# Batch-by-batch folding in a Fourier-mixing and low-rank-mixer kernel: where the first batch's narrow sums run, how the second batch's sine groups and channel step are computed, and when the third batch is folded

## The chip, the cores and the metric

The kernel runs on one core of a Trainium2 chip. A core has a matrix engine (TensorE, "PE" in the profile; its weight loads are listed as "PEld"), a vector engine (VectorE, "DVE"), an activation engine (ScalarE, "ACT"), a general engine (GpSimd, "POOL") and a queue engine (SyncE, "SP"). Each engine works through its own list of instructions in order; semaphores make one wait for another. Matmul results go to PSUM, everything else lives in SBUF. The metric is the device time of one execution in microseconds (us).

## The reference

```python
def _attn_ref(x):                       # x: 8 x 3136 x 256
    X = np.fft.fft(x, axis=1)
    X = np.fft.fft(X, axis=2)
    return X.real.astype(np.float32)

def _moe_ref(x, U, V, w_ch1, w_ch2):    # U: 3136 x 32, V: 32 x 3136
    xt = x.transpose(0, 2, 1)
    h = xt @ U @ V
    u = x + h.transpose(0, 2, 1)
    ch = np.maximum(u @ w_ch1, 0.0) @ w_ch2     # 256 -> 1024 -> 256
    return (u + ch).astype(np.float32)
```

The output is `_moe_ref` of `_attn_ref(x)`: the real part of a two-dimensional Fourier transform of each of eight batches, then a low-rank mixing along the sequence and a two-layer product along the channels, both with a residual.

## The kernel before

**Batches.** Each of the 8 batches has 3136 rows. Its inputs (`xf`, the rows read forwards, and `xr`, read backwards; 98 partitions of 8 rows each, plus row 0 in partition 98) are folded by `fold(b)`: `along_d` (line 386) adds or subtracts mirrored channels into `EOF_` and `EOR_`, `mirror` (L395) joins these into `EOS`, `half` (L399) joins the two halves of the sequence into `G[b % 2][par]`. The next batch's loads (`load_half`, L55, L86, L101, L103) are issued by GpSimd from inside the fold, since they overwrite what the fold has read. From batch 1 to batch 7 a fold has 16 steps, or 14 where there is no next batch to load. For batches 0 and 1 there is also a narrow column (channel 0, handled alone; L392).

`transform(b)` then runs the sequence transform: eight calls of `seq`, one for each parity `par`, type `typ` (1 is cosine, 0 sine) and input parity `pn`. A plain call is four matmuls of 425 columns (L485); with `pn == 0` ScalarE evicts the result to an `ev` tile (L489), with `pn == 1` VectorE adds and subtracts it and `ev` into the tiles `A` (cosine) and `B` (sine) (L492, L500, L504). `halves` (L425 to L437) replaces a `pn == 0` call: its four matmuls (L430) have 229 columns only, because the outputs mirror each other, and two VectorE instructions (L436, L437) make the full `ev` from the two sums. `quarters` (L439 to L464) goes one step further and is used from batch 2 (`B0`).

Then comes the channel step, from `A` and `B` to `S` and `T`. `chan` (L628) makes one of the two with two matmuls of 392 columns (L631 from `A`, L633 from `B`) and one copy out of PSUM (L635, ScalarE, or VectorE where `dve` is set). `even_ch` and `odd_ch` make both at once: one product of `A` (L643), evicted by ScalarE to `evd` (L645), one product of `B` (L652), and two VectorE instructions that add and subtract (L654). With them goes `across` (L664, L666), which copies 64 rows of `A` into `VA`, tied behind the last Relu on ScalarE; without them `last_row` (L684) writes a single row of `VA` on VectorE. Batch 0 and 1 use `chan`, batches 2 to 7 `even_ch` and `odd_ch`.

`first_channel` (through `narrow`, L545 to L577) makes a narrow row of `VA` for batches 0 and 1: 16 matmuls (L556), an eviction to `evc` (L560), and six sums (L570, L573, L574), on VectorE for batch 0 and on GpSimd for batch 1. On GpSimd it needs a second eviction, `evo` (L563), because there the sums read SBUF. The same routine makes the narrow rows of batches 2 to 7 together (`column_steps`). All tiles `ev`, `evc`, `evo` and `evd` share four buffers; all PSUM tiles of these steps share three (`dft`).

**Chunks.** The second stage works on 49 chunks of 512 rows. `front(c)` adds a product of `TA` and `VA` (L709) to `S` or `T` and writes `u` (L725, two or more VectorE instructions); a DMA transposes it. `first_product(c, j)` (L735, two matmuls of 512 columns, Relu on ScalarE L737) runs for j = 0 to 7; `second_product(c-1, t)` (L751, eight matmuls of 256 columns) for t = 0 to 3, with three VectorE additions to the output tile after each pair (L757, L759, L760).

**Order.** Step `8 * c + j` runs one first product, on odd j one second product of the chunk before, then what `due` lists for this step, and at j = 3 the front of the next chunk. `spread(steps, lo, hi)` puts a fold or a transform evenly over the steps lo to hi. Batch 1's first output row lies in chunk 6, whose front is issued at step 43; batch 2's in chunk 12 (step 91). Up to the end of chunk 0 the order of each engine is as written; from chunk 1 on a planner orders the instructions by what it takes to be ready, while the fold's instructions keep their place (`pin`).

## Time and profile before

| what | value |
|---|---|
| time, median of 3 runs | 447.03 us (446.45 to 447.28) |
| time of the profiled execution | 447.31 us |
| its span in the profile | 445.2 us |
| mean granted TensorE clock | 1.00 |
| VectorE busy | 353.1 us |
| ScalarE busy | 297.5 us |
| GpSimd busy | 85.7 us |

The span runs from the first to the last instruction that the profile shows; 2.1 us of the execution's own time lie outside it. A line of a timeline gives the start, the duration, the engine, the source line, the operation, output and inputs, shapes, and the number of instructions merged into the line; in square brackets, how long the engine stood idle before it and what ended that. TensorE's matmuls overlap, so a matmul's listed duration is longer than its share of the engine: that share is the distance from one start to the next.

### The profile page before, as it was taken

How to read it: one execution, taken by the hardware profiler on the slowest of the kernel's cores; microseconds unless marked ns; L12 is line 12 of the kernel's file. 1: busy time of each engine (PE TensorE's matmuls, PEld its weight loads, DVE VectorE, ACT ScalarE, POOL GpSimd, SP SyncE). 2: the span in 40 equal slices, each digit the busy share in tenths (PEclk: the TensorE clock that was granted, in tenths of full speed). 3: DMA queues.
4: the chain of work that ended last, by engine and by line, in shares of the span. 5: the costliest groups of instructions: out<-in, count | busy, mean ns of one | idle time of the engine just before them, and what ended most of it. 6: DMA issues, size and time to landing. Idle time of an engine off the chain costs nothing.

```text
span 445.2 us, 8087 instructions
## 1 busy us (share of the span) xinstructions
PE 435.7 (98%) x2960; PEld 316.4 (71%) x3012; DVE 353.1 (79%) x838; ACT 297.5 (67%) x564; POOL 85.7 (19%) x144
## 2 busy tenths in 40 slices
PE   8999999999999999999999999999999999999997
PEld 6456766776677777777777777777777777777775
DVE  8879998888998799878998789878998776443433
ACT  8857747565885669655875569655876569656562
POOL 8973217300931002300211001300000000000000
PEclk9999999999999999999999999999999999999999
DMA  7998997995199437674779537782333332434343
GB/s 133 210 230 180 229 173 117 245 153 103 49 230 265 120 106 216 190 171 73 157 203 222 108 103 216 196 167 71 95 119 95 91 100 73 117 97 121 93 125 112
DMA packets 103249, 65.36 MB, mean 147 GB/s; under 512 B 73806, under 2 KB 99624, under 8 KB 100464
## 3 DMA queue, kind: packets, MB, share of 16 engines
q1 hardware_dynamic: 97528, 39.10, 40.1%
q0 software_dynamic: 5664, 25.75, 21.6%
q8 instruction: 23, 0.38, 0.3%
q14 instruction: 16, 0.13, 0.1%
q10 hardware_dynamic: 18, 0.00, 0.0%
HBM read 29.33 MB, written 25.69 MB: 124 GB/s over the span
## 4 chain that ended last, share of the span: by engine, by line
PE 91%; DVE 2%; DMA 2%; issue 1%; POOL 1%; ACT 1%; DVEq 0%; POOLq 0%
PE p L751 38%; PE p L735 35%; PE pt L485 6%; PE ph L709 5%; DMA xb<-in_x_dram,xidx 2%; PE ptq L446 2%; PE pst L643 1%; PE pst L652 1%; PE m L850 1%; PE ptc L556 1%; ACT h L737 0%; DVE eor L386 0%; PE pst L631 0%; DVE eof L386 0%; PE pst L633 0%
## 5 line engine op out<-in xcount | busy, mean ns | idle before, releaser
L737 ACT ACTIVATE h<-p 128x512 bf16<-128x512 f32 x392 | 222.0, 597 | 119.5 <-PE p L735 107.3
L735 PE MATMUL p<-u,w 128*128 128x512 bf16 x735 | 209.3, 379 | 1.2 <-DVE B L500 0.2
L751 PE MATMUL p<-w,h 128*128 128x256 bf16 x1568 | 203.0, 273 | 1.4
L751 PEld LDWEIGHTS <-h 128*128 128x128 bf16 x1568 | 153.2, 98 | 50.4 <-DVE o L760 0.3
L735 PEld LDWEIGHTS <-w 128*128 128x128 bf16 x784 | 106.1, 144 | 35.1 <-issue 2.0
L757 DVE TENSOR_TENSOR o<-p,ut 128x4 f32<-128x4 f32 (+1 forms) x100 | 16.2, 162 | 54.9 <-PE p L751 53.3
L759 DVE TENSOR_TENSOR o<-p,ut 128x254 f32<-128x254 f32 (+1 forms) x100 | 40.5, 405 | 0.0
L760 DVE TENSOR_TENSOR o<-p,ut 128x254 f32<-128x254 f32 (+1 forms) x100 | 40.5, 405 | 0.0
L468 POOL TENSOR_TENSOR tab<-tf 128x64 bf16<-128x64 f32 x7 | 3.1, 440 | 179.2 <-DVE tf L492 179.1
L386 DVE TENSOR_TENSOR eof<-xf 99x1024 bf16<-99x1024 f32 x28 | 35.8, 1293 | 0.0
L386 DVE TENSOR_TENSOR eor<-xr 99x1024 bf16<-99x1024 f32 x28 | 34.8, 1247 | 0.0
L725 DVE TENSOR_TENSOR u<-ph,S 128x512 bf16<-128x512 f32 (+23 forms) x63 | 34.3, 553 | 0.0
L725 DVE TENSOR_TENSOR u<-ph,T 128x512 bf16<-128x512 f32 (+23 forms) x63 | 34.2, 553 | 0.0
L55 POOL DMA_INDIRECT xf<-in_x_dram,xidx x14 | 17.3, 1234 | 62.0 <-DVE eof L386 48.5
L709 PE MATMUL ph<-va,ta 128*128 128x512 bf16 (+15 forms) x124 | 28.6, 328 | 0.3
L485 PEld LDWEIGHTS <-g 98*128 98x128 bf16 (+1 forms) x152 | 14.7, 98 | 13.1 <-issue 0.7
L395 DVE TENSOR_TENSOR eos<-eof,eor 99x1024 bf16<-99x1024 bf16 (+1 forms) x28 | 19.2, 702 | 0.0
L654 DVE TENSOR_TENSOR S<-evd,pst 128x392 bf16<-128x392 f32 (+1 forms) x24 | 13.5, 564 | 6.4 <-PE pst L652 4.1
L485 PE MATMUL pt<-tabs,g 98*128 98x425 bf16 x80 | 17.6, 344 | 0.0
L457 DVE TENSOR_TENSOR ev<-ptq,ex 128x131 f32<-128x131 f32 (+1 forms) x24 | 6.9, 289 | 12.9 <-ACT ex L450 12.9
L399 DVE TENSOR_TENSOR g<-eos 99x2048 bf16<-99x2048 bf16 (+1 forms) x14 | 16.9, 1217 | 0.0
L485 PE MATMUL pt<-tabc,g 98*128 98x425 bf16 x72 | 15.5, 344 | 0.0
(198 smaller groups left out, 381.0 us busy)
## 6 DMA issues: line engine op xcount, KB each, us to landing
out_dram<-o SPq DMA_DIRECT2D x48, 512.0 KB
xr<-in_x_dram POOLq DMA_DIRECT2D x14, 784.0 KB, 8.2
xb<-in_x_dram POOLq DMA_DIRECT2D x2, 392.0 KB, 7.9
ut<-u SPq DMA_TRANSPOSE x49
w<-in_moe_w_ch_dram POOLq DMA_DIRECT2D x1, 512.0 KB
out_dram<-o SPq DMA_DIRECT2D x4, 128.0 KB
va<-in_moe_V_dram POOLq DMA_DIRECT2D x2, 196.0 KB
w<-in_moe_w_ch_dram POOLq DMA_DIRECT2D x1, 256.0 KB, 7.2
```

The costliest lines, as they stand in the source:

```text
L55: nc.gpsimd.indirect_dma_start(out_, None, bass.AP(t.tensor, t.offset, [[w, rows], [1, w]]), bass.IndirectOffsetOnAxis(idx, 0), element_of ...
L386: pin(nc.vector.tensor_tensor(dst[:, a, :, part * P:(part + 1) * P].rearrange("p i (k t) -> p i k t", k=2), lo, hi, op=AL.subtract if part ...
L395: pin(nc.vector.tensor_tensor(EOS[:, a, :, cols], EOF_[:, a, :, cols], EOR_[:, a, ::-1][:, :, cols], op=op))
L399: pin(nc.vector.tensor_tensor(G[b % 2][par][:, :, cols], EOS[:, 0, :, cols], EOS[:, 1, :, cols], op=AL.add if par == 0 else AL.subtract))
L485: nc.tensor.matmul(pt[:], g[:kp(i), i, P * typ:P * (typ + 1)], tabs[typ][:kp(i), i, par, :], start=(n == 0), stop=(n == NI // 2 - 1))
L709: nc.tensor.matmul(ph, TA[b % 2][:k, s * P:(s + 1) * P], VA[b % 2][:k, lo:hi], start=start, stop=True)
L725: nc.vector.tensor_tensor(u[:, s, col:col + hi - lo], ph[:, col:col + hi - lo], src, op=AL.add)
L735: nc.tensor.matmul(p1[:], W1[:, s, j::JT], k["u"][:, s, :], start=(s == 0), stop=(s == 1))
L737: LAST[0] = nc.scalar.activation(k["h"][:, j, :], p1[:], AF.Relu)
L751: nc.tensor.matmul(p2[:, t % w, :], h[:, j, rs], W2[:, j, :], start=(j == 0), stop=(j == JT - 1))
L759: nc.vector.tensor_tensor(o[:, ts, 1:P], p2[:, :w, 1:P], ut[:, ts, 1:P], op=AL.add)
L760: nc.vector.tensor_tensor(o[:, ts, P + 1:D], p2[:, :w, P + 1:D], ut[:, tT, P - 1:0:-1], op=AL.add)
```

## The change

Four things change together.

- The first batch's narrow sums go from VectorE to GpSimd (`eng=nc.gpsimd`), which adds the `evo` eviction and moves all six sums, two of them (the late ones) to behind the start of chunk 0.
- The second batch's two sine groups (`typ == 0`) with `pn == 0` go through `halves`, as its cosine groups did already.
- The second batch's channel step uses `even_ch`, `odd_ch` and `across` in place of eight `chan` calls; `last_row(1)` goes, the low product of batch 1 reads all 128 rows of `TA` and `VA`, and one of the two memsets of `VA[1]` goes.
- Batch 1's fold is spread over steps 2 to 21 (was 4 to 23) and its transform over 21 to 42 (was 23 to 42); batch 2's fold over 30 to 58 (was 24 to 55) and its transform over 60 to 90 (was 57 to 90).

```diff
-        if pn == 0 and (b >= B0 or b == 1 and typ == 1):
+        if pn == 0 and b:
             (quarters if b >= B0 else halves)(d, g, par, typ)
             return
...
-        k = P if b >= B0 else 2 * R + 1
+        k = P if b else 2 * R + 1
...
             for ch in range(4):
-                for h in range(2):
-                    yield lambda ch=ch, h=h: chan(b, ch * 392 + (1 if ch else 0),
-                                                  (ch + 1) * 392 + 1, h)
+                yield lambda ch=ch: (even_ch(b, ch), across(b, ch, False))
+                yield lambda ch=ch: (odd_ch(b, ch), across(b, ch, True))
             yield from row[3:]
-            yield lambda: (lowrank(b), last_row(b))
+            yield lambda: lowrank(b)
             return
...
-    narrow_0 = list(first_channel(0, tag=("p2", 2), late=late))
+    narrow_0 = list(first_channel(0, tag=("p2", 2), late=late, eng=nc.gpsimd))
...
-    va_zeros(1)
+    nc.gpsimd.memset(VA[1][R:2 * R].bitcast(I32), 0)
...
         if b == 1:
-            spread(list(fold(b)), 4, 23)
-            spread(list(transform(b)), 23, hi)
+            spread(list(fold(b)), 2, 21)
+            spread(list(transform(b)), 21, hi)
         else:
-            spread(list(fold(b)), hi - 66, hi - 35)
-            spread(list(transform(b)), hi - 33, hi)
+            lag = 3 if b == B0 else 0
+            spread(list(fold(b)), hi - 66 + 2 * lag, hi - 35 + lag)
+            spread(list(transform(b)), hi - 33 + lag, hi)
```

## The prediction

> **What bounds the kernel now.** I read the busy shares and the chain of waits first, then busy time by stretches, then the timelines where the change works.
>
> ```profile
> PE 435.7 (98%) x2960; PEld 316.4 (71%) x3012; DVE 353.1 (79%) x838; ACT 297.5 (67%) x564; POOL 85.7 (19%) x144
> PE 91%; DVE 2%; DMA 2%; issue 1%; POOL 1%; ACT 1%; DVEq 0%; POOLq 0%
> ```
>
> TensorE is busy for 98% of the span and makes 91% of the chain that ends last. So a matmul column less is time less, as long as nothing starves TensorE. What could starve it is VectorE, third of the busy columns here (the columns are stretch, its length, then busy us of PE, PEld, DVE, ACT, POOL with counts, clock, DMA share, GB/s):
>
> ```profile
> 54.00:62.00 8.00, 7.95 (x54) 5.40 (x54) 7.86 (x18) 4.40 (x9) 0.07 (x1) 1.00 1.13 211
> 62.00:70.00 8.00, 7.79 (x61) 5.02 (x61) 7.42 (x17) 3.92 (x9) 2.53 (x4) 1.00 0.70 140
> 70.00:78.00 8.00, 7.80 (x51) 5.38 (x50) 6.86 (x12) 6.55 (x15) 7.76 (x9) 1.00 0.70 114
> 86.00:94.00 8.00, 7.95 (x58) 6.10 (x58) 5.83 (x12) 4.72 (x9) 0.00 (x0) 1.00 1.05 204
> 118.00:126.00 8.00, 7.88 (x54) 5.76 (x53) 8.00 (x15) 6.89 (x14) 6.98 (x7) 1.00 0.52 123
> ```
>
> From 54 to 70 us, in batch 1's transform, VectorE has 0.7 us free in 16; at 118 it has none; at 86 it has 2.2 of 8. ScalarE has room everywhere. TensorE's clock is 1.00 throughout. The change takes work from TensorE in the stretch where VectorE is full and gives VectorE more: that is the question of this case.
>
> **TensorE: what goes.** Distances from one start to the next:
>
> ```profile
> 54.62 0.56 PE L430 MATMUL pth<-tabc,g 98*128 98x229 bf16 x4
> 55.02 0.88 PE L485 MATMUL pt<-tabc,g 98*128 98x425 bf16 x4
> 55.74 0.89 PE L485 MATMUL pt<-tabs,g 98*128 98x425 bf16 x4
> ...
> 68.15 0.33 PE L631 MATMUL pst<-A,mc 128*128 128x393 bf16 x1
> 68.32 0.33 PE L633 MATMUL pst<-B,msn 128*128 128x393 bf16 x1
> 68.49 0.59 PE L735 MATMUL p<-u,w 128*128 128x512 bf16 x2
> ```
>
> A plain group of four takes 55.74 - 55.02 = 0.72 us, a `halves` group 55.02 - 54.62 = 0.40. Two sine groups: 2 x 0.32 = 0.64. A channel product takes 68.32 - 68.15 = 0.17; eight `chan` calls are 16 of them, the even and odd products 8: 8 x 0.17 = 1.36. Together 2.00 us. The low product over 128 instead of 65 rows costs nothing: its columns stay, and columns set the time of every row above.
>
> **VectorE, ScalarE, GpSimd: what comes.**
>
> ```profile
> L654 DVE TENSOR_TENSOR S<-evd,pst 128x392 bf16<-128x392 f32 x18 | 10.1, 563 | 4.0 <-ACT h L737 2.0 <-PE pst L652 1.8
> L437 DVE TENSOR_TENSOR ev<-pth,ev 128x229 f32<-128x229 f32 x2 | 0.8, 398 | 0.0
> L684 DVE TENSOR_TENSOR va<-S,T 1x1567 bf16<-1x1567 bf16 x2 | 1.9, 968 | 0.9 <-ACT T L635 0.9
> L645 ACT COPY evd<-pst 128x392 f32<-128x392 f32 x18 | 8.7, 481 | 0.1
> L664 ACT COPY va<-A 64x392 bf16<-64x392 bf16 x18 | 9.3, 515 | 0.4
> L395 DVE TENSOR_TENSOR eos<-eof,eor 99x1024 bf16<-99x1024 bf16 x26 | 17.9, 703 | 0.0
> L759 DVE TENSOR_TENSOR o<-p,ut 128x254 f32<-128x254 f32 x96 | 39.4, 411 | 0.0
> ```
>
> VectorE in batch 1: 8 additions and subtractions x 0.563 = +4.5; two each of L436 and L437, at most 4 x 0.398 = +1.6; `last_row(1)` -1.0: +5.1 us. The last two rows are used further down. ScalarE: 4 evictions x 0.481 + 8 copies x 0.515 = 6.0, for eight copies of 392 columns out of PSUM, 8 x 0.481 = 3.8: +2.2 us. In the 70 to 78 stretch it has 1.45 of 8 free and more on both sides, so I put it at nothing; without that room it would delay Relus by up to 2.2.
>
> Against the +5.1 stands batch 2's fold, moved away. Before step 43, where batch 1 is first needed, the old spread (24 to 55, 16 steps) puts 11 fold steps, the new one (30 to 58) 8: three `along_d` fewer, at 1.2 to 1.8 us each:
>
> ```profile
> 69.46 1.02 POOL L573 TENSOR_TENSOR va<-evo,evc 1x393 bf16<-1x393 f32 x1
> 70.44 1.47 POOL L574 TENSOR_TENSOR va<-evc,evo 1x392 bf16<-1x392 f32 x1
> ...
> 73.89 1.82 DVE L386 TENSOR_TENSOR eof<-xf 99x1024 bf16<-99x1024 f32 x1
> 76.57 0.97 DVE L684 TENSOR_TENSOR va<-S,T 1x1567 bf16<-1x1567 bf16 x1 [0.85 <-ACT T L635]
> 80.02 1.21 DVE L386 TENSOR_TENSOR eor<-xr 99x1024 bf16<-99x1024 f32 x1
> ```
>
> That is -3.6 to -5.4, and -1.2 for the two late sums that leave VectorE at 32.75. So the sum up to step 43 is between +0.3 and -1.5 us. It has to come out 1.8 us sooner than now, because the handover has no slack:
>
> ```profile
> 83.81 0.61 DVE L725 TENSOR_TENSOR u<-ph,T 128x448 bf16<-128x448 f32 x1
> 84.60 0.81 PE L735 MATMUL p<-u,w 128*128 128x512 bf16 x3
> ```
>
> Chunk 6's `u` is done at 84.42, TensorE takes it at 84.60: 0.18 us, and TensorE will ask 2.0 earlier. VectorE's idle 0.85 before `last_row(1)` goes with that instruction. -0.85 and -0.6 (the middle of the sum) are 1.45 of the 1.8 wanted; I charge the rest, +0.3.
>
> One line above gives a price that the change pays: a GpSimd sum takes 1.02 alone and 1.47 beside VectorE's fold, and an `along_d` 1.82 beside GpSimd against 1.21 alone. The Trainium skill ("SBUF — State Buffer", Who interferes with whom) makes it a rule against this change: a VectorE instruction with two SBUF inputs and a GpSimd instruction that reads SBUF exclude each other, and the later one blocks fully. By that rule each overlap would cost up to a whole 1.0 to 1.2 us; the rows show 0.45 and 0.6, so the trace agrees in kind and gives half the price. By the rule's price the forecast would be about 1 us higher.
>
> **The start.** The narrow sums leave VectorE ahead of its join at 28.87 (four) and at 32.75 (two).
>
> ```profile
> 25.53 3.02 PE pt L485 x16
> 28.87 0.04 DVE tab L468
> ...
> 25.58 0.51 ACT L560 COPY evc<-ptc 64x425 f32<-64x425 f32 x1 [0.48 <-PE ptc L556]
> ...
> 30.07 0.59 PE L709 MATMUL pu<-va,ta 65*128 65x512 bf16 x2
> 38.80 0.67 POOL L86 DMA_DIRECT2D xr<-in_x_dram  x1 [7.51 <-DVE eor L386]
> ...
> L570 POOL TENSOR_TENSOR tf<-evo,evc 1x32 f32<-1x32 f32 x2 | 0.7, 368 | 5.5 <-ACT evo L563 5.4
> ```
>
> The first four gain nothing: the chain runs through TensorE's sixteen matmuls to 28.55. They must not cost either: the evictions, at 25.58 and, new, 26.1, end at 26.6; GpSimd needs 0.37 + 1.02 + 0.37 us to the end of the second short sum, 28.4, which the join at 28.87 reads; the second row is done at 29.4, and L709 reads it at 30.07. The slack is 0.5 to 0.7 us; if it is gone, each tenth of lateness costs a tenth. VectorE's sums of that moment read PSUM and only one tile in SBUF, so I expect no stretching. What waits behind on GpSimd (memsets, `ME`, the narrow casts of L392, batch 2's first load) shifts by the six sums, 4 x 1.02 + 2 x 0.37 = 4.8 us; that load now stands 7.51 us idle ahead of its issue at 38.80, which covers it.
>
> But the fold's two earlier steps are not free. Steps 2 and 3 lie ahead of chunk 1's front, in the part whose order is as written:
>
> ```profile
> 32.75 1.22 DVE L574 TENSOR_TENSOR va<-evc,ptc 1x392 bf16<-1x392 f32 x2
> 35.30 0.68 DVE L725 TENSOR_TENSOR u<-ph,T 128x512 bf16<-128x512 f32 x1
> 35.90 2.35 DVE L386 TENSOR_TENSOR eor<-xr 99x1024 bf16<-99x1024 f32 x2
> ...
> 36.66 0.33 PE L631 MATMUL pst<-A,mc 128*128 128x392 bf16 x1
> ```
>
> Two `along_d` (2.35) now stand before `u`, in place of two sums (1.22): `u` ends 1.13 later, at 37.1. TensorE wants it at 36.23, two 512-column matmuls ahead of the last row (0.17 x 512 / 393 = 0.22 each). Bounds: 0 (the planner fills the hole with other matmuls) to 0.9, and with both `along_d` stretched by the moved sums' company 0.9 + 1.2 = 2.1. I take +0.3, nearer the filled case, because from chunk 1 on channel products and second products stand ready.
>
> **Batch 2 later.** The old trace loses time where batch 3's fold meets GpSimd's column sums:
>
> ```profile
> 113.04 3.25 DVE L386 TENSOR_TENSOR eof<-xf 99x1024 bf16<-99x1024 f32 x2
> ...
> 117.30 0.33 PE L643 MATMUL pst<-A,me 128*128 128x392 bf16 x1 [0.36 <-DVE T L654]
> ...
> xr<-in_x_dram POOLq DMA_DIRECT2D x14, 784.0 KB, 8.2
> ```
>
> TensorE idles 0.36 us. That fold does not move. Batch 2's transform does, from 57 to 60, into this full stretch by about one `seq`: between -0.4 (the meeting shifts apart) and +1.1 (one more stall of a `seq`'s two VectorE sums); I take 0. Its fold then ends some 3 steps later; 94 us is its deadline and the stretch at 86 has 2.2 us free. The eight loads of batch 3 that it issues move by 4 to 6 steps behind GpSimd's narrow sums; they land in 8.2 us (the last row) and are first read at 113: nothing; without those 20 us of lead the wait would be VectorE's.
>
> **The sum:** 447.31 - 2.00 + 0.3 (handover) + 0.3 (start) = 445.91 for the profiled execution; that execution is 0.28 above the median of the runs shown, so 445.63. Two gains were set to nothing in it: the 0.36 at 117, and what TensorE misses of the 62 to 78 stretch (15.59 busy of 16, 0.4 us), where the ScalarE copies out of PSUM that go are thickest. I count half of them, 0.4, and put the forecast at 445.2 us.
>
> **The rivals.**
> *All of it and the stalls too:* the start's hole is filled, the handover holds, and both of these stalls go in full. 447.03 - 2.0 - 0.8 = 444.2. For it: those stalls are VectorE's and ScalarE's evictions, which change. Against: VectorE has no more room than before.
> *No change:* the start costs its upper 0.9 and the handover slips by 1.0: 447.03 - 2.0 + 1.9 = 446.9. It is what a zero slack at both places would do.
> *VectorE becomes the bound in steps 31 to 42 (slower).* The sum up to step 43 balances, but its end does not: these 11 steps now hold 8 x 0.563 = 4.5 of S and T, four `along_d` of 1.2 that GpSimd's sums stretch by 0.6 each (7.2), two mirrors (1.4), output additions (nearly three pairs of 2 x 0.41, 2.3) and `u` (about three of 0.68, 2.0): 17.4 us. TensorE's work there is 11 steps of two 512-column and four 256-column matmuls (2 x 0.22 + 4 x 0.11 = 0.88), 1.4 for the channels and some 0.7 for fronts and low rank: 11.8 us. Odd products keep their PSUM tile until both sums are done, and the fold keeps its place, so TensorE would wait. Of the 5.6 about 1.6 (two pairs of output additions) fit into the output sums' two buffers: +4.0, 447.03 - 2.0 + 4.0 = 449.0. It makes the kernel slower from 2.9 us of new stalls on. Against it: the planner can let late channel products wait, as only the first 448 rows are due at step 43.
>
> **How the numbers follow.** A measurement of this kernel tells about 0.2% (0.9 us) from no change. Forecast (444.5 to 446.1): 0.55; all of it and stalls: 0.12; no change: 0.14; slower: 0.19. Faster 0.67, same 0.14, slower 0.19. The range runs from 443.9 to 448.2, into the slower case; the forecast's own is 444.5 to 446.1.
>
> **What would show it.** Right: L430 twice as often, L485 fewer by 8, L631 and L633 only batch 0's; chunk 6's `u` and TensorE within 0.3 us near 82.6; the sixteen matmuls' end still near 28.5. Wrong: TensorE idle before chunk 1's first product, or before L643 and L652 between 60 and 80; ScalarE waiting on GpSimd's hold on `evc` and `evo`; idle over 1 us at 105 to 130.

## The result: the changed kernel is 4.1% slower

| what | before | after |
|---|---|---|
| time, median | 447.02 us (446.45 to 447.73) | 464.84 us (464.31 to 467.61) |
| ratio after / before | | 1.0413, interval 1.0383 to 1.0442 |
| time of the profiled execution | 447.31 us | 464.86 us |
| its span | 445.2 us | 463.1 us |
| mean granted TensorE clock | 1.00 | 0.985 |

The forecast was 445.2 us, in a range up to 448.2. The time lies 17.8 us above the kernel before and far outside that range. Medians and brackets take all executions of a kernel; a ratio can leave out executions more than 1.5% above the fastest.

The page of the kernel after, busy time and chain of waits by engine:

```profile
PE 437.4 (94%) x2951; PEld 317.2 (68%) x3004; DVE 352.7 (76%) x843; ACT 300.6 (65%) x569; POOL 91.6 (20%) x149
PE 80%; DVE 7%; DMA 4%; POOL 4%; issue 2%; ACT 2%; SPq 0%; DVEq 0%; POOLq 0%; ACTq 0%
```

TensorE is busy for as long as before (437.4 against 435.7 us, some of it at a lower clock), but its share of the chain fell from 91% to 80%: the new time is waiting. Where it waits can be read from one thing that both traces have, the start of the first Relu (`h`, L737) of each chunk. The table gives that start less its start in the kernel before; the column of the kernel after is followed by two experiments that are told further down. Within a column, only the changes from row to row count: the first Relu of a profiled execution came up to 1.1 us apart in kernels with the same prologue (e7 and e17).

| first Relu of chunk | before, at us | after | e6 | e18 |
|---|---|---|---|---|
| 0 | 31.86 | +11.70 | -0.73 | -1.00 |
| 1 | 37.02 | +11.91 | -0.74 | -0.99 |
| 3 | 53.86 | +13.40 | -0.73 | -0.99 |
| 5 | 77.69 | +11.65 | +1.86 | -1.79 |
| 7 | 92.67 | +11.45 | +1.11 | -2.05 |
| 8 | 102.17 | +10.70 | +1.11 | -2.25 |
| 9 | 112.79 | +16.29 | +1.10 | -2.27 |
| 11 | 129.64 | +17.39 | +1.11 | -2.21 |
| 48 | 431.86 | +17.39 | +1.11 | -2.18 |

So the loss is made in three places: 11.7 us before the first chunk; between chunks 0 and 7 only 0.25 is won, though 2.0 us of matmul columns are gone (another 0.75 comes back between chunks 7 and 8); 6.7 us between chunks 8 and 11. From chunk 11 on both kernels run alike.

**The start.** Four timelines of the kernel after (ScalarE, TensorE, GpSimd, VectorE), the same place as the prediction's rows at 25.53 to 30.07:

```profile
25.96 0.51 ACT L563 COPY evo<-ptc 64x425 f32<-64x425 f32 x1
...
28.45 0.38 PE L963 MATMUL pu<-B,msn 128*128 128x512 bf16 x1
39.40 0.40 PE L678 MATMUL ptt<-msn,tab 128*128 128x256 bf16 x1 [10.58 <-DVE tab L468]
...
41.55 0.43 PE L631 MATMUL pst<-A,mc 128*128 128x273 bf16 x1
41.78 0.43 PE L633 MATMUL pst<-B,msn 128*128 128x273 bf16 x1
...
37.44 0.24 POOL L570 TENSOR_TENSOR tf<-evo,evc 1x32 f32<-1x32 f32 x1 [11.20 <-DMA xf<-in_x_dram,xidx]
...
39.12 0.22 DVE L468 TENSOR_TENSOR tab<-tf 128x64 bf16<-128x64 f32 x1 [10.43 <-POOL tf L570]
```

`evo` is ready at 26.47 and TensorE's sixteen matmuls end at 28.5, both as predicted. But the first GpSimd sum, 0.24 us long, starts at 37.44: GpSimd stood idle for 11.20 us, and what ended that is a DMA, the indirect load (gather) of `xf`. The join at L468 and TensorE wait behind it. The chain of waits of the kernel after names the same transfer:

```profile
19.98 17.21 DMA xf<-in_x_dram,xidx
```

It is batch 1's gather, issued on GpSimd in two halves at 17.99 and 19.98, the second landing at 37.2. The narrow sum doesn't read `xf`. Busy time by stretches of the kernel after (columns as in the prediction):

```profile
30.00:40.00 10.00, 0.60 (x3) 0.39 (x4) 0.72 (x2) 0.00 (x0) 2.33 (x4) 0.66 0.44 110
40.00:50.00 10.00, 9.61 (x42) 5.04 (x41) 7.67 (x11) 6.94 (x15) 6.85 (x18) 0.83 0.17 35
120.00:130.00 10.00, 7.82 (x54) 4.83 (x56) 5.95 (x22) 4.92 (x11) 0.86 (x2) 0.83 0.33 81
```

The granted clock was 1.00 everywhere before; here it is 0.66 in the hole's stretch and 0.83 after it. The two products of 273 columns at 41.55 and 41.78 stand 0.23 us apart, where 0.17 for 393 columns makes 0.12 at full clock. The Trainium skill ("TensorE: Matmul & The Clock Gate", Why this matters for your kernels) warns of idle gaps of over some 3 us for this reason; the trace agrees, at holes of 10.6 and 4.0 us.

**Chunks 8 to 11.** SyncE's queue, ScalarE and TensorE of the kernel after:

```profile
103.95 6.14 SPq L539 DMA_DIRECT2D cr<-in_x_dram  x2
...
117.32 1.70 SPq L539 DMA_DIRECT2D cr<-in_x_dram  x2
...
120.95 0.27 ACT L590 CAST cb<-cr 99x96 bf16<-99x96 f32 x1 [4.28 <-DMA cr<-in_x_dram]
...
122.13 1.60 PE L485 MATMUL pt<-tabc,g 98*128 98x425 bf16 x4 [3.96 <-ACT h L737]
```

The last column load of the kernel before, for comparison:

```profile
101.43 1.70 SPq L539 DMA_DIRECT2D cr<-in_x_dram  x2
```

The small loads of the narrow columns (`cf`, `cr`, L539) go through SyncE's queue; the last is issued at 117.32 in place of 101.43, 4.4 us more than the 11.45 by which everything is late there, and an issue of two took 6.14 us, close to the last one, where it took 1.70. ScalarE stands at L590 for 4.28 us waiting for them, the Relus stand behind it, and TensorE is idle for 4.0 us, and the clock of the stretch is 0.83. In this stretch batch 3's loads, which follow batch 2's later fold, are new: their gathers are issued at 87.58 and 96.58, before the change at 61.93 and 80.94. The kernel before has a slow issue beside these loads too, but early enough that nothing waits for it:

```profile
85.76 4.58 SPq L539 DMA_DIRECT2D cr<-in_x_dram  x2
```

**Batch 1's channel step.** GpSimd, VectorE, ScalarE and TensorE of the kernel after:

```profile
78.88 2.09 POOL L574 TENSOR_TENSOR va<-evc,evo 1x392 bf16<-1x392 f32 x1
...
83.31 1.01 POOL L574 TENSOR_TENSOR va<-evc,evo 1x392 bf16<-1x392 f32 x1
...
78.86 1.22 DVE L386 TENSOR_TENSOR eof<-xf 99x1024 bf16<-99x1024 f32 x1
...
84.04 0.52 ACT L666 COPY va<-A 64x392 bf16<-64x392 bf16 x1
84.58 0.49 ACT L645 COPY evd<-pst 128x392 f32<-128x392 f32 x1
...
85.12 0.38 PE L709 MATMUL ph<-va,ta 65*128 65x512 bf16 x1 [1.45 <-ACT evd L645]
```

TensorE waits 1.45 us for ScalarE's third eviction to `evd`. Two things stand ahead of that eviction, and most of the experiments are about telling them apart: `evd` shares four buffers with `evc` and `evo`, which GpSimd's six sums hold until 84.32; and ScalarE, which works in order, is busy with a copy across until 84.56.

### The profile page after: what moved, and what is told of

Its sections match the earlier page's. It is cut to its first block, busy times and chain, and to the rows that moved or that the text cites. A ratio compares the mean times of both kernels' runs of the same rounds, so it can differ in the third digit from the quotient of the medians.

```text
span 463.1 us, 8091 instructions
## 1 busy us (share of the span) xinstructions
PE 437.4 (94%) x2951; PEld 317.2 (68%) x3004; DVE 352.7 (76%) x843; ACT 300.6 (65%) x569; POOL 91.6 (20%) x149
## 4 chain that ended last, share of the span: by engine, by line
PE 80%; DVE 7%; DMA 4%; POOL 4%; issue 2%; ACT 2%; SPq 0%; DVEq 0%; POOLq 0%; ACTq 0%
PE p L751 35%; PE p L735 31%; PE pt L485 5%; PE ph L709 4%; DMA xf<-in_x_dram,xidx 4%; PE ptq L446 2%; DVE eof L386 1%; PE pst L643 1%; DVE eor L386 1%; DVE u L725 1%; ACT h L737 1%; PE pst L652 1%; DVE eos L395 1%; DMA cr<-in_x_dram 1%; DVE g L399 1%
## 5 line engine op out<-in xcount | busy, mean ns | idle before, releaser
L737 ACT ACTIVATE h<-p 128x512 bf16<-128x512 f32 x392 | 221.5, 597 | 118.9 <-PE p L735 99.2
L468 POOL TENSOR_TENSOR tab<-tf 128x64 bf16<-128x64 f32 x7 | 3.9, 564 | 153.3 <-DVE tf L492 153.2
L386 DVE TENSOR_TENSOR eof<-xf 99x1024 bf16<-99x1024 f32 x28 | 34.2, 1235 | 0.0
L55 POOL DMA_INDIRECT xf<-in_x_dram,xidx x14 | 19.3, 1380 | 61.3 <-DVE eof L386 56.4
L709 PE MATMUL ph<-va,ta 128*128 128x512 bf16 (+15 forms) x124 | 28.6, 328 | 1.6 <-ACT evd L645 1.5
L654 DVE TENSOR_TENSOR S<-evd,pst 128x392 bf16<-128x392 f32 (+1 forms) x28 | 15.8, 565 | 8.1 <-PE pst L652 4.1
L485 PE MATMUL pt<-tabs,g 98*128 98x425 bf16 x72 | 15.8, 344 | 0.1
```

The source lines that it names most:

```text
L55: nc.gpsimd.indirect_dma_start(out_, None, bass.AP(t.tensor, t.offset, [[w, rows], [1, w]]), bass.IndirectOffsetOnAxis(idx, 0), element_of ...
L386: pin(nc.vector.tensor_tensor(dst[:, a, :, part * P:(part + 1) * P].rearrange("p i (k t) -> p i k t", k=2), lo, hi, op=AL.subtract if part ...
L485: nc.tensor.matmul(pt[:], g[:kp(i), i, P * typ:P * (typ + 1)], tabs[typ][:kp(i), i, par, :], start=(n == 0), stop=(n == NI // 2 - 1))
L709: nc.tensor.matmul(ph, TA[b % 2][:k, s * P:(s + 1) * P], VA[b % 2][:k, lo:hi], start=start, stop=True)
L737: LAST[0] = nc.scalar.activation(k["h"][:, j, :], p1[:], AF.Relu)
```

## The experiments

Times are medians with lowest and highest in brackets, ratios against the kernel before on the same chip, whose median lay between 446.93 and 447.24 us. Line numbers beyond 563 are some lines higher in the kernels that add lines (L645 is L648 in e13 to e18, L737 is L740 or L747).

### The start: is it GpSimd's sums, and what do they wait for?

**e1**, the changed kernel with batch 0's narrow sums back on VectorE:

```diff
-    narrow_0 = list(first_channel(0, tag=("p2", 2), late=late, eng=nc.gpsimd))
+    narrow_0 = list(first_channel(0, tag=("p2", 2), late=late))
```

> The changed kernel with the first batch's narrow sums back on VectorE; all else as changed. Theory (the first GpSimd sum waits until batch 1's gathers have landed, and the join, the low-rank product and all of the second stage wait for it): the 10.7 us hole before the low-rank product goes, and with it some 1.2 us of matmuls at a lowered clock behind it: 464.8 - 11.9 = 452.9 us (451.5 to 454.5). Rival A (VectorE's load in batch 1 is what costs, as the slower case of the prediction had it): the hole's time comes back later as VectorE has 1.2 us more: 463 to 466. What is left over 447.0 then belongs to the other three parts.

Measured: 453.87 us (449.55 to 458.86), ratio 1.0079 (1.0050 to 1.0107). 11.0 us are back in the medians (13.0 without the two longest executions of e1, 456.77 and 458.86), and the first Relu comes at 31.68.

**e2**, the reverse: the kernel before with that one edit.

> The kernel before with the first batch's narrow sums alone on GpSimd. Theory: the same hole, 447.0 + 11.9 = 458.9 us (457 to 460.5), first GpSimd sum at about 37.4 us, a granted clock below 1 behind it. Rival A: within 1 us of 447.0.

Measured: 458.59 us (458.25 to 459.52), ratio 1.0253 (1.0236 to 1.0270): this edit by itself costs 11.4 us. GpSimd of e2:

```profile
37.91 0.24 POOL L570 TENSOR_TENSOR tf<-evo,evc 1x32 f32<-1x32 f32 x1 [11.69 <-DMA xf<-in_x_dram,xidx]
```

**e3**, the changed kernel with batch 1's `xf` loaded by a plain DMA on the same engine, rows in rising order, so that no gather of it is in flight (the mirror of batch 1 is then not the reference's):

```diff
     def load_second(a):
         load_r(1, a)
-        load_f(1, a)
+        nc.gpsimd.dma_start(out=xf[:PQ, a].rearrange("p i d -> p (i d)"),
+                            in_=bass.AP(x.tensor, x.offset + (S + a * HALF + 1) * D,
+                                        [[8 * D, PQ], [1, 8 * D]]))
```

> The changed kernel, with batch 1's forward rows loaded by a plain GpSimd DMA in ascending order instead of the gather that turns the order round; same bytes, issued from the same place. Batch 1's output is then not the reference's. Theory (the wait is for gathers in flight): the first GpSimd sum starts at 26 to 28 us as soon as both evictions are done, the hole is under 1.5 us, 451.5 to 455 us. Rival B (GpSimd waits for any load of its own in flight, or the sums are slow there for another reason): the sum starts after 36 us again, 463 to 466 us.

Measured: 451.41 us (449.79 to 452.67), ratio 1.0104 (1.0078 to 1.0131). The first sum of e3:

```profile
26.54 0.24 POOL L570 TENSOR_TENSOR tf<-evo,evc 1x32 f32<-1x32 f32 x1 [0.62 <-ACT evo L563]
```

**e4**, the changed kernel with its gathers, but the four narrow rows evicted to partition 0 of a free tile, from where GpSimd reads them:

```diff
+            if late is None:
...
+            if late is not None:
+                v = EOS[0:1].rearrange("p a i d -> p (a i d)").bitcast(FP32)
+                t["r"] = [v[:, k * QW:(k + 1) * QW] for k in range(4)]
+                for k in range(4):
+                    g = 2 * (k % 2) + k // 2
+                    nc.scalar.copy(t["r"][k], pt[g * R:g * R + 1])
+                return
...
+            if late is not None:
+                e, o = t["r"][2 * par], t["r"][2 * par + 1]
```

> The changed kernel, gathers kept, with the four narrow rows of batch 0 evicted one by one to partition 0 (four copies of 1 x 425 into an idle stretch of EOS) instead of to partitions 64 to 127. In the program the first GpSimd sum then waits for no gather; it did with its inputs at partition 64. Theory (the wait comes with GpSimd reading from a partition other than 0 while gathers are in flight): first sum at 26 to 28.5 us, hole under 2 us, 452 to 455.5 us. Rival B: first sum after 36 us, 463 to 466 us.

Measured: 454.96 us (451.07 to 456.78), ratio 1.0188 (1.0165 to 1.0211). The first sum of e4:

```profile
26.46 0.24 POOL L581 TENSOR_TENSOR tf<-eos 1x32 f32<-1x32 f32 x1 [0.26 <-ACT eos L567]
```

The four runs settle the place and the condition: the sum waits when gathers are in flight and it reads rows that don't start at partition 0; without the gather (e3) or from partition 0 with the gathers (e4) it starts as soon as its data is there. e4 changes the tile along with the partition; but in the kernel after, GpSimd's instructions at 21.19 to 26.24 read three other tiles from partition 0 while both gathers are in flight, and none of them waits. The wait is in the program: the sum's own list of waits holds the semaphores of the gathers issued on GpSimd ahead of it. Why the program carries it for some partitions only was not found. e5 and e18 show the same wait once more, at other places, and it can already be found in the kernel before, at batch 1's first sum:

```profile
68.91 0.49 POOL L570 TENSOR_TENSOR tf<-evo,evc 1x32 f32<-1x32 f32 x1 [5.41 <-ACT evo L563]
```

This sum's list holds the gather issued at 61.93 as well, which landed 6.6 us later, at 68.5. `evo` was done at 68.83 and is named, since it came last, by 0.3 us.

### Chunks 8 to 11: what does the later fold of batch 2 cost?

**e8**, the kernel before with `lag` alone:

```diff
-            spread(list(fold(b)), hi - 66, hi - 35)
-            spread(list(transform(b)), hi - 33, hi)
+            lag = 3 if b == B0 else 0
+            spread(list(fold(b)), hi - 66 + 2 * lag, hi - 35 + lag)
+            spread(list(transform(b)), hi - 33 + lag, hi)
```

> The kernel before with only the third batch's fold and transform later (30 to 58, 60 to 90). Theory: a hole before L590, and 449 to 453 us, with runs further apart than those of the kernel before. Rival E (the lag alone is harmless, and costs only together with the fuller VectorE of the changed batch 1): 446.5 to 447.8 us.

Measured: 451.00 us (448.49 to 455.99), ratio 1.0127 (1.0068 to 1.0187). The profiled execution is the fastest of them and still has a hole of 1.71 us in TensorE's work, up to 107.57, with ScalarE idle for 2.03 us ahead of L590. The spread between executions grows with it, to 7.5 us here and 9.3 in e1, against 1.3 for the kernel before; other kernels with the lag spread less (2.9 in e3, 3.3 in the kernel after).

**e11**, e8 with the column loads issued sooner:

```diff
-            due.setdefault(8 + 2 * n, []).append(step)
+            due.setdefault(8 + 7 * n // 4, []).append(step)
```

> As the eighth experiment (before, with the third batch's fold and transform later), and the 28 column loads issued at steps 8 to 55 instead of 8 to 62. Theory (batch 3's later loads delay the column loads, and L590 waits for the last of them): the hole at L590 goes, 447 to 448.5 us, runs close together. Rival H (the lag costs by the denser transform, not by the loads): 449.5 to 453 as without this edit.

Measured: 449.01 us (447.53 to 451.00), ratio 1.0047 (1.0026 to 1.0069). That misses both expectations. The wait at L590 is gone, and another has come, 2.3 us of TensorE at 97. The waits of e11 between 94 and 102 us:

```profile
DVE o L757 <- DMA ut<-u: 4.3, 1, 4.3
PE pt L485 <- DVE u L725: 2.3, 1, 2.3
```

(waiting engine and line, what for, total us, times, longest.) VectorE's output sum now waits 4.3 us for the transpose of a chunk, which uses SyncE's queue too. This fits a price of the lag that is paid on that queue: earlier loads take 2.0 us off e8's median and don't bring the kernel before back.

**e5**, e1 without the lag (`lag = 0`):

> As the first experiment (narrow sums on VectorE), and batch 2's fold and transform back at steps 24 to 55 and 57 to 90. Theory (the later fold issues batch 3's loads into the time of the column loads, which come in late, and ScalarE, in order, waits for them at L590): the hole of 3.8 us near 108 us and the 1.5 us behind it go, 453.9 - 5.3 = 448.6 us (447.3 to 450), and the runs lie closer together than the 449.6 to 458.9 of the first experiment. Rival C (the hole is VectorE's load in batch 1 and its backlog, wherever batch 2 lies): 452 to 456 us.

Measured: 451.25 us (449.98 to 452.48), ratio 1.0098 (1.0070 to 1.0131), which misses the expected 447.3 to 450. GpSimd, ScalarE and TensorE of e5:

```profile
71.00 0.24 POOL L570 TENSOR_TENSOR tf<-evo,evc 1x32 f32<-1x32 f32 x1 [5.24 <-DMA xf<-in_x_dram,xidx]
...
76.56 0.48 ACT L645 COPY evd<-pst 128x392 f32<-128x392 f32 x1 [2.13 <-POOL va L574]
...
77.10 0.38 PE L709 MATMUL ph<-va,ta 65*128 65x512 bf16 x1 [2.53 <-ACT evd L645]
```

By the Relu starts, e1 loses 5.8 us between chunks 7 and 11 and e5 none; but e5 loses 3.9 between chunks 0 and 7, where e1 loses 1.2. In this pair of executions the lag costs 5.8 us where it acts and gives 2.7 back in batch 1's channel step, which without it has batch 2's fold and batch 3's gathers beside it. The first row shows how a gather acts there: `evo` was done at 69.06, the sum waits until 71.00 for batch 3's gather, which it doesn't read, and GpSimd gives its buffers back as much later. The cost of the lag differs between executions: between chunks 7 and 11 the others with it lose 5.9 (after), 2.2 (e3), 2.6 (e4) and 2.1 us (e8). So what it costs net can't be told from e1 and e5: their medians are 2.6 us apart, but without e1's two longest executions only 0.6, and the intervals of their ratios overlap.

### Batch 1: where do the 2.0 us of matmul columns go?

**e6**, e5 with the old spreads of batch 1 as well (`fold` 4 to 23, `transform` 23 to `hi`): the sine halves and the even and odd products are all that is left of the change.

> As the one before, and batch 1's fold and transform back at steps 4 to 23 and 23 to 42: what is left of the change is the sine groups through halves and the even and odd channel products. Theory: the idle before chunk 1's first product (1.8 us in the first experiment) goes, 2.0 us of matmul columns are saved, and one hole of 1.6 us near 73 us stays, where ScalarE's third evd eviction waits until GpSimd has given the evc buffer back: 447.2 - 2.0 + 1.6 = 446.8 us (446 to 448). Rival C: 449 to 454 us.

Measured: 448.88 us (448.25 to 449.17), ratio 1.0045 (1.0028 to 1.0061), above the expected 446 to 448. The earlier spreads cost 2.4 us here, where batch 0's sums are on VectorE. The hole of 1.4 us (1.27 and 0.15) that e1 and e5 have ahead of chunk 1 goes with them; VectorE and TensorE of e1 there:

```profile
35.57 1.22 DVE L386 TENSOR_TENSOR eor<-xr 99x1024 bf16<-99x1024 f32 x1
36.70 0.68 DVE L725 TENSOR_TENSOR u<-ph,S 128x512 bf16<-128x512 f32 x1
...
37.45 0.44 PE L735 MATMUL p<-u,w 128*128 128x512 bf16 x1 [1.27 <-DVE u L725]
```

But 1.8 us are still lost against the kernel before, with 2.0 us less of columns.

**e9**, the kernel before with the sine halves alone:

```diff
-        if pn == 0 and (b >= B0 or b == 1 and typ == 1):
+        if pn == 0 and b:
```

> The kernel before with only the second batch's two sine groups through halves. Theory: 0.64 us of matmul columns go and VectorE gets 1.5 us more in a stretch where it is full: 446.5 us (446.1 to 447.2), the only part of the change that can win by itself. Rival: VectorE's 1.5 us come out in full behind it, 447.6 to 448.6.

Measured: 446.77 us (445.89 to 447.57), ratio 0.9994 (0.9985 to 1.0003): no measurable difference, so the loss of e6 comes with the channel step.

**e10**, e6 without `across` in batch 1 (rows 64 and up of its `VA` are zeros):

```diff
-                yield lambda ch=ch: (even_ch(b, ch), across(b, ch, False))
-                yield lambda ch=ch: (odd_ch(b, ch), across(b, ch, True))
+                yield lambda ch=ch: even_ch(b, ch)
+                yield lambda ch=ch: odd_ch(b, ch)
...
+    nc.gpsimd.memset(VA[1][2 * R:].bitcast(I32), 0)
```

> As the sixth experiment (only even and odd products and halves), without the eight across copies of batch 1 on ScalarE; 64 rows of VA[1] are zeros instead, so two channels of batch 1's output are not the reference's. Theory F (ScalarE, with 2.2 us more in 69 to 80 us, is what TensorE waits for there: Relus stand behind across and evd): 446.4 us (445.6 to 447.4), 2 us or more below the 448.9 with them. Rival G (VectorE's additions and subtractions, which hold the odd products' PSUM tiles): 448.2 to 449.2.

Measured: 449.87 us (448.40 to 450.37), ratio 1.0062 (1.0043 to 1.0081): in the median slower than e6, with eight copies less, and above what either theory expected. GpSimd, ScalarE and TensorE of e10:

```profile
68.27 0.96 POOL L570 TENSOR_TENSOR tf<-evo,evc 1x32 f32<-1x32 f32 x1 [5.21 <-ACT evo L563]
...
72.97 1.01 POOL L574 TENSOR_TENSOR va<-evc,evo 1x392 bf16<-1x392 f32 x1
...
74.02 0.49 ACT L645 COPY evd<-pst 128x392 f32<-128x392 f32 x1 [2.47 <-POOL va L574]
...
74.55 0.38 PE L709 MATMUL ph<-va,ta 65*128 65x512 bf16 x1 [2.59 <-ACT evd L645]
```

The six sums take from 68.27 to 73.98 and hold two of the four buffers; the third `evd` needs one and starts at 74.02. ScalarE, without the copies, is there sooner and stands at the head of its list for 2.47 us, with the Relus behind it. The clock falls to 0.87 and 0.91 in the stretches from 70 to 78 and from 78 to 86 us. In one of e10's four executions it stayed at 1.00; that one took 448.40 us, so most of e10's distance from e6 may be the clock's.

**e7**, e6 with the whole narrow row of batch 1 ahead of its sequence transform, so that the sums are over before the channel step:

```diff
+        if b < B0:
+            row = list(first_channel(b, eng=nc.gpsimd))
+            yield from row
         for par in range(2):
...
-            row = list(first_channel(b, eng=nc.gpsimd))
-            yield from row[:2]
-            yield lambda: (row[2](), joined(b))
+            yield lambda: joined(b)
...
-            yield from row[3:]
```

> As the one before, with batch 1's narrow row (products, both evictions, six sums, turning) ahead of its eight sequence groups instead of behind them, so that evc and evo are free again when the evd tiles ask for buffers. Theory: the 1.6 us hole goes, 445.2 us (444.3 to 446.2), below the kernel before. Rival D (the hole is VectorE's, which has to free the PSUM tiles of the odd products): within 0.6 us of the kernel without this edit.

Measured: 448.11 us (447.59 to 448.93), ratio 1.0028 (1.0016 to 1.0041), far from the expected 445.2. ScalarE and TensorE of e7:

```profile
74.35 0.52 ACT L664 COPY va<-A 64x392 bf16<-64x392 bf16 x1
74.89 0.60 ACT L737 ACTIVATE h<-p 128x512 bf16<-128x512 f32 x1
75.52 0.52 ACT L666 COPY va<-A 64x392 bf16<-64x392 bf16 x1
76.06 0.49 ACT L645 COPY evd<-pst 128x392 f32<-128x392 f32 x1
...
76.59 0.33 PE L652 MATMUL pst<-B,msn 128*128 128x392 bf16 x1 [1.61 <-ACT evd L645]
```

At this place no buffer is missing, and the eviction is late because two copies across and a Relu stand ahead of it. (A second hole, of 0.92 us at 64 us, is of the kind that e12 shows below.)

Putting the row first also leaves something out, which the experiment didn't intend. GpSimd's short sums put channel 0's share of the low-rank product into row 0 of `tf`, and batch 1's sine groups write over all 128 rows of the same part of `tf`. In the kernel before they come ahead of the sums, here behind them (GpSimd and VectorE of e7):

```profile
60.43 0.24 POOL L570 TENSOR_TENSOR tf<-evo,evc 1x32 f32<-1x32 f32 x1
...
70.09 0.18 DVE L492 TENSOR_TENSOR tf<-pt,ev 128x32 f32<-128x32 f32 x1
```

So in e7, e12, e14, e15 and e18 channel 0 is missing from batch 1's low-rank product. No instruction is missing, so their times still tell where the waits are.

**e12**, e7 without `across`:

> The even and odd products and the sine halves, with batch 1's narrow row ahead of its sequence transform, and without the eight copies across (rows 64 to 127 of batch 1's VA are zeros, so two channels of batch 1 are not the reference's). Theory H (two things eat the 2.0 us of matmul columns in turn: GpSimd's hold on the narrow row's eviction tiles, and the copies across ahead of an eviction in ScalarE's order; each run so far took away only one of them): both are gone, TensorE idles under 1 us between 60 and 80, and the time is 445.0 to 446.2. Theory I (what is left is VectorE: the sine groups' two sums and eight additions and subtractions at 0.56 us, with batch 2's fold beside them): the hole moves to where VectorE is late, TensorE idles 1.5 us or more between 60 and 80, and the time stays at 447 to 448.5.

Measured: 446.73 us (446.50 to 447.13), ratio 0.9995 (0.9986 to 1.0004). The hole at 75 us is gone; one at 65 us, 1.52 us of ScalarE and 1.33 of TensorE, stays. GpSimd, ScalarE and TensorE of e12:

```profile
62.94 2.00 POOL L574 TENSOR_TENSOR va<-evc,evo 1x392 bf16<-1x392 f32 x1
...
64.97 0.35 ACT L433 COPY ev<-pth 128x229 f32<-128x229 f32 x1 [1.52 <-POOL va L574]
...
66.07 0.88 PE L485 MATMUL pt<-tabc,g 98*128 98x425 bf16 x4 [1.33 <-DVE ev L437]
```

TensorE names VectorE, VectorE had waited for ScalarE's `ev`, and ScalarE for the buffer that the last sum held: the hold again, at the sine halves. So neither expectation was met in full: the two named causes were both at work, and one of them had only moved.

**e13** to **e17** take the hold away: `evc` and `evo` of the narrow rows that GpSimd sums get two tiles of their own in a pool with room.

```diff
-            t["ev"] = wp.tile([P, QW], FP32, tag="ev", name="evc", bufs=4)
+            if eng is nc.gpsimd:
+                t["ev"] = cp.tile([P, QW], FP32, tag="evc", name="evc", bufs=1)
+            else:
+                t["ev"] = wp.tile([P, QW], FP32, tag="ev", name="evc", bufs=4)
...
-                t["pt"] = wp.tile([P, QW], FP32, tag="ev", name="evo", bufs=4)
+                t["pt"] = cp.tile([P, QW], FP32, tag="evo", name="evo", bufs=1)
```

e13 is e6 with these tiles, e14 is e7, e15 is e12, e16 the kernel before, e17 is e10.

> e6 (even and odd products and sine halves only) with evc and evo of batch 1's narrow row in two tiles of their own, so that GpSimd's late sums hold none of the four buffers that evd and ev rotate through. Theory G (the hold is what eats the gain): the hole ahead of L652 or L709 at 70 to 78 us goes, ScalarE's L645 waits for no GpSimd instruction, and the time falls from e6's 448.88 to 446.0 to 447.2. Theory F (the copies across on ScalarE) and theory V (VectorE): 448.3 to 449.2, TensorE's idle between 60 and 80 us stays near 3 us with another releaser.

> The same with the narrow row ahead of batch 1's sequence transform (e7 with tiles of their own). Theory G: the 1.08 hole at 64 us, in which ScalarE's eviction of a sine half waited for GpSimd, goes; the 1.78 hole at 75 us, an eviction behind two copies across, stays: 448.11 - 1.1 = 446.8 to 447.3. Theory F: the same, as F names the other hole. If VectorE is behind the 64 us hole: 447.8 to 448.4.

> e12 with tiles of their own (no copies across: two channels of batch 1 are not the reference's). Both named causes are gone. G and F together: TensorE's idle between 60 and 80 us falls under 0.6 us and the time from 446.73 to 445.0 to 445.6, which is the matmul columns' gain of 2.0 less some 0.3. Theory V: an idle of 1 us or more stays behind a VectorE instruction and the time stays over 446.2.

> The kernel before with the same two tiles of their own and nothing else. Before has no even and odd products in batch 1, its sums on GpSimd come behind the transform, and its trace shows no hole from them: all theories 446.6 to 447.2. If it is faster than 446.4, the tiles are worth something by themselves and e13 to e15 have to be read against it.

> e13 without the copies across (two channels of batch 1 are not the reference's), the narrow row in its old place behind the sequence transform. If the copies are worth 1.5 us wherever the row stands: 448.7 - 1.5 = 447.2, in 446.9 to 447.6, and the hole-by-Relu pattern of e13 at 70 to 80 us goes. If the place of the row decides and the copies only add to it: 448.2 to 448.9. In e10, the same without tiles of its own, GpSimd's hold stopped ScalarE for 2.5 us; here it cannot.

Measured: e13 448.70 us (448.40 to 448.95), ratio 1.0034 (1.0022 to 1.0046); e14 447.91 (447.20 to 448.49), 1.0018 (1.0009 to 1.0027); e15 446.32 (445.80 to 447.05), 0.9982 (0.9973 to 0.9991); e16 447.20 (446.76 to 447.45), 1.0000 (0.9991 to 1.0009); e17 446.23 (445.88 to 446.69), 0.9980 (0.9971 to 0.9989). The tiles by themselves do nothing (e16, as expected). The other four missed their expectations: e13 and e14 are above theory G's ranges, e15 is above 445.0 to 445.6 though its largest hole is down to 0.50 us, and e17 is below both of its ranges. The eight medians around the channel step, side by side:

| narrow row, copies across | four shared buffers | tiles of their own |
|---|---|---|
| behind the transform, copies on ScalarE | e6 448.88 | e13 448.70 |
| behind the transform, no copies | e10 449.87 | e17 446.23 |
| first, copies on ScalarE | e7 448.11 | e14 447.91 |
| first, no copies | e12 446.73 | e15 446.32 |

In the upper half, taking away the hold alone gives 0.2 us (within the spread of the runs), taking away the copies alone costs 1.0, and taking away both gives 2.65. In the lower half, with the sums over before the channel step, the copies alone are worth 1.4, the hold alone 0.2 and both 1.8. Each covers for the other: ScalarE is late with the eviction either because it has copies ahead of it or because it has no buffer. e13's expectation by theory G (the hold is everything) fell; in its place TensorE waited in eight pieces of 0.1 to 0.65 us, 2.1 us in all, mostly for Relus. Busy time between 62 and 86 us in e13 and, below, in e17:

```profile
62.00:86.00 24.00, 21.86 (x152) 14.71 (x151) 23.84 (x51) 17.34 (x34) 14.24 (x17) 1.00 0.76 163
```

```profile
62.00:86.00 24.00, 23.73 (x171) 16.56 (x170) 24.00 (x52) 12.71 (x26) 14.35 (x17) 1.00 0.77 167
```

ScalarE has 4.6 us less to do in e17, and TensorE, busy for 21.86 of 24 us in e13, is busy for 23.73. VectorE is full in both: the change makes it the busiest engine of this stretch, but that is not what held TensorE up in e13.

**e18**, e14 with batch 1's copies across on GpSimd; like e14 it leaves channel 0 out of batch 1's low-rank product, and nothing else:

```diff
+        if b == 1:
+            if back:
+                lo, hi = max(lo, 1), min(hi, HALF)
+                nc.gpsimd.tensor_copy(to[:, S - hi + 1:S - lo + 1], src[:, hi - 1:lo - 1:-1])
+            else:
+                nc.gpsimd.tensor_copy(to[:, lo:hi], src[:, lo:hi])
+            return
         with tc.issue_after(LAST[0].ins):
```

> e14 with batch 1's eight copies across on GpSimd in place of ScalarE; the output is complete. Theory F (ScalarE's order): the 1.78 hole at 75 us goes, as in e15, and the time is 446.1 to 446.9. The rival is the wait on gathers: GpSimd reads rows 64 and up, so the copies wait for the gather issued at 66.5 us and hold up batch 3's next one; if chunk 6's low product at 84 us then waits for them, 448 to 452.

Measured: 446.03 us (444.82 to 446.92), ratio 0.9978 (0.9969 to 0.9988). That is just under the expected 446.1 to 446.9, and 1.1 us below the kernel before in the medians (447.17 beside it). It has all of the kernel's work except that one overwritten row; a version that keeps the row was not run. GpSimd of e18:

```profile
65.85 1.65 POOL L55 DMA_INDIRECT xf<-in_x_dram,xidx  x1 [0.32 <-POOL va L625]
...
72.95 0.57 POOL L669 COPY va<-A 64x393 bf16<-64x393 bf16 x1 [3.09 <-DMA xf<-in_x_dram,xidx]
...
77.22 0.52 POOL L667 COPY va<-A 64x391 bf16<-64x391 bf16 x1
```

The first copy reads rows from partition 64 on, and waits for a gather that it has nothing to do with: the start's wait again. Here it is just covered: the last copy is done at 77.74, chunk 6's low product reads these rows from 77.99 on, and TensorE has no idle time over 0.21 us between 58 and 90. The expectation had put that product at 84.

## Why the prediction was wrong, point by point

**The narrow sums on GpSimd.** The step that failed is the sentence "the first four gain nothing ... GpSimd needs 0.37 + 1.02 + 0.37 us to the end of the second short sum, 28.4 ... the slack is 0.5 to 0.7 us". No duration was longer than it assumed: `evo` was ready at 26.47, the sums took 0.24 and 1.01. The start was wrong: it waited 11.2 us for batch 1's gathers. Without that wait (e3) the product that needs the second row, L709, starts at 30.33, against 30.07 in the kernel before. With the lower clock behind the hole it is 11 to 13 of the 17.8 us (e1), and 11.4 by itself (e2). In the trace of before the wait was hidden: GpSimd's sums of batch 1 wait for a gather there too, but `evo` came 0.3 us after it and is named. The form of the error was in the argument, though: what the sums would wait for was taken from the data they read, and GpSimd was looked at as a queue of durations. Its outstanding loads, issued at 17.99 and 19.98 for a fold much later, were not looked at.

**Batch 2 later.** The step "they land in 8.2 us ... and are first read at 113: nothing" failed, and with it the bound of +1.1. It looked at who reads the loads; the cost lies with the other loads that are in flight at the time, the columns' on SyncE's queue. It is 2.1 to 5.9 us where it acts, from execution to execution; on the kernel before it is 3.9 in the median (1.5 to 9, e8), and net of what it gives back in batch 1 it can't be told (e1, e5). That it is a contention between batch 3's loads and the columns' fits the issues of 6.14 us (after) and 4.58 us (before) beside these loads and e11's moved wait, but it is not shown: which of the DMA's resources is short was not separated.

**The start's +0.3.** Its reason and its size were right: with the sums on GpSimd and no wait, e3 and e4 lose 0.44 and 0.45 us between the first Relus of chunks 0 and 1. e1 loses 1.6 there, but it has the two late sums back on VectorE, so that the two `along_d` stand ahead of chunk 1's `u` in addition to them and not in their place; this is no case of the prediction.

**The matmul columns, -2.00.** The instructions went as counted. The gain did not arrive: with all other parts undone (e6) the kernel is still 1.8 us slower than before. The step that failed is ScalarE, "+2.2 us ... I put it at nothing; without that room it would delay Relus by up to 2.2". In e6 and e13 it does that, since ScalarE's busy share is not what counts: the copies stand in order ahead of an eviction that TensorE waits for. The hold of `evc` and `evo` was named among the things that would show the prediction wrong, but had no term and no chance. Both together are 2.65 us (e6 to e17).

**The handover, +0.3.** No loss is seen there: between chunks 5 and 7 the kernel after keeps its distance (+11.65, +11.45). But TensorE did not come 2.0 us sooner, as the term assumes, so it was not put to the test.

**The price of an overlap on VectorE's and GpSimd's shared reads.** The forecast took 0.45 to 0.6 us from its rows, against the rule of the Trainium skill ("SBUF — State Buffer", Who interferes with whom) that the later one blocks fully. The sum at 78.88 began 0.02 us after an `along_d` of 1.22 and took 2.09 in place of 1.02; it was blocked for nearly the whole of it. The forecast's "half the price" misread its rows: they overlapped in part. When the sum at 70.44 began, 0.59 us of a `mirror` were left, and it lost 0.45; when the `along_d` at 73.89 began, 0.75 us of a GpSimd sum were left, and it lost 0.61. In all three rows the later one lost most of what was left of the earlier one, which is the rule's size. It decided nothing here.

**The rivals.** The slower one had the right sign and the wrong mechanism: VectorE does become full (24.00 of 24 us in e17), and TensorE is served all the same.

What stays open: e17 and e18 win 0.9 and 1.1 of the 2.0 us, with no hole over 0.42 us left in TensorE's list; the rest is in small pieces that were not assigned. e17 leaves out the copies across and e18 channel 0's share, so no kernel here that computes everything has been shown to be faster than the kernel before.

## What to carry to other kernels

Before work is moved to GpSimd, list what that engine has in flight at the new place, indirect loads above all, and not only what the moved instruction reads; keep such work clear of them in time. When tiles of one buffer group are read by a slow engine, its last read is the next eviction's start, and an in-order engine passes that wait on to everything behind it, so taking away one of two causes may show nothing or a loss. A transfer that is moved is priced against the transfers it will then run beside, whoever reads it.

## What was not expected of the hardware

- GpSimd's sums and copies that read from partition 64 waited for indirect loads in flight on their engine: 11.20 us (after), 11.69 (e2), 3.09 (e18), and in e5 1.9 us beyond their data; not from partition 0 (0.26, e4), nor beside plain loads (0.62, e3).
- A hole of 2.6 us in TensorE's work already came with a granted clock of 0.87 and 0.91 in the 16 us around and after it (e10), while a hole of 2.5 us in e5 left it at 1.00 there; of e10's four executions one kept a mean clock of 1.00, of e5's four two fell to 0.995 and 0.996. The Trainium skill's 3 us ("TensorE: Matmul & The Clock Gate", Why this matters for your kernels) is not a sharp edge in these runs.
- Kernels with the lag vary by 2.9 to 9.3 us between executions (e3, e1), the kernel before by 1.3.
